# Attention and two MoE layers on one core: the first MoE in three passes instead of four

## The chip, the cores and the metric

The kernel runs on one core of a Trainium2 chip. The metric is the device time of one execution in microseconds (us), here the median of three runs. The engines are named as in the profile: PE (TensorE, matmuls), PEld (its weight loads), DVE (VectorE), ACT (ScalarE), POOL (GpSimd), and SP, whose queue issues nearly all DMA transfers.

## What is computed

Block-causal attention over 4 batches of 576 tokens with 8 heads of 64, then a gated layer over all 2304 tokens, then four experts whose outputs are weighted by probabilities. All of it is float32 (the first layer's weights come as float64).

```python
def _attn_ref(q, k, v):                    # q, k, v: (4, 8, 576, 64)
    scores = scale * np.matmul(q, k.transpose(0, 1, 3, 2))
    mask = block_i >= block_j              # blocks of 64 positions
    scores = np.where(mask, scores, -1000000000.0)
    ...                                    # softmax over the last axis
    return np.matmul(attn, v)

def _moe_ref(x, w_gate, w_val, w_out):     # x: (2304, 512), d_ff 1536
    gate = 1.0 / (1.0 + np.exp(-(x @ w_gate)))
    return gate * (x @ w_val) @ w_out

def _moe2_ref(x, domain_probs, w1, w2):    # 4 experts, 512 -> 1024 -> 512
    p = domain_probs / (domain_probs.sum(-1, keepdims=True) + 1e-09)
    for e in range(E):
        out += p[:, e:e + 1] * (np.maximum(x @ w1[e], 0.0) @ w2[e])
    return out
```

## The kernel before

**Numbers.** A float32 factor is split into a high and a low part (`split_sb`: one engine rounds, another subtracts), and a product is three matmuls: high by high, high by low, low by high. First products are done by a Winograd scheme: 2 x 2 blocks of x and of the weights, seven block products instead of eight, with sums of blocks made beforehand.

**Stages.** (1) Attention, `attn_items` (L152), makes a queue of small steps for each batch and pair of heads: loads, transposes of q and k (`prep_tr`, L224), scores, softmax, transposes of the probabilities, product with v (`pv_both`, L511). It writes its result to DRAM tiles `x_d[batch, "a" or "b", pair]`: "a" has the first 256 tokens of the batch, "b" the other 320. Batches 0 and 1 are of kind N (scores from unsplit factors), 2 and 3 of kind F (split factors).
(2) The first MoE, in `NP1` = 4 passes p of 576 tokens, each two halves t of `TH1` = 288. Twelve steps f run over blocks of 128 gate and 128 value columns (d_ff 1536). A step has one first product, `l1_1` (L788): seven block products of 6 matmuls in the order 1, 2, 6, 5, 7, 4, 3, into banks c1 and c2, with copies (`snap`), additions and the gate behind them, and at its end the tile g. Two steps share a second product, `l2_1` (L865): 4 output blocks x 2 halves x 2 steps x 3 matmuls, added into x2 tiles by DVE (L884), in banks "lo" and, from pass 2 on, "o". It runs among the matmuls of the next two steps. After the last step the x2 tiles are written to DRAM (`x2_d`).
(3) The second MoE, in three passes of 768 tokens (halves of 384): first products `l1_items`, second products `l2_items` (pass 0, 512 columns) and `l2s_items` (later passes, 256 columns).

**What a pass needs.** `x1_prep(p)` (L736) or, for passes 2 and 3, `x1_early` loads the blocks of x of batch p, makes four sums on POOL and splits seven blocks into the xc tiles. `w1_load(f)` loads the split weights of a step: tiles a, b, c of tag "wg" (6 of them in a ring) and d. In pass 0 the weights come in float64; `conv_items(f)` makes them and stores them to DRAM. `wo_get` does the same for w_out (4 whole tiles). All tiles of the first MoE lie in one pool, `moe1`; a pool for pass 2's early x (`x1b`) lies where attention was.

**Order.** The outer loop over passes (L1297) lists the steps' items, puts loads between them as side items, merges them with the second product of the two steps before (`_merge`), and before each item asks for attention up to a place: `attn_to(A1[p] + (A1[p+1] - A1[p]) * share / PACE1)`, where a place counts batches (1.05 is batch 0 and a twentieth of batch 1). With `A1 = [1.05, 2.3, 4, 4, 4]` pass 0 takes batch 1 and 0.3 of batch 2, pass 1 the rest. This order is a priority: the Tile framework schedules the instructions of each engine by it and by a timeline of its own, so that work stated later can run earlier where its inputs and tiles are free.

Of the kernel before, what the change touches and what calls it, by code (L numbers as in the profile page):

```python
# [21 lines left out]
A1 = [1.05, 2.3, 4, 4, 4]  # L22
PACE1 = 0.9
GB = 4
UB = 1
# [9 lines left out]
W2B = 4  # L35
FIRSTP = 1
W1B = 5
PRE0, PRE1 = 0.4, 0.9
# [24 lines left out]
def attention_moe_moe_kernel(  # L63
# [72 lines left out]
    moe1 = tc.alloc_tile_pool(name="moe1", bufs=1)  # L136
# [15 lines left out]
    def attn_items(segs):  # L152
# [6 lines left out]
        QTS = KTS = {"N": range(5), "F": range(5)}  # L159

        def nat_of(g):
            return pairs[g][3] != "F"
# [20 lines left out]
        def load(g, nm, src, c0, c1):  # L183
# [14 lines left out]
            for x, (y, z) in enumerate(((nm, src),) if nm == "v" else (("k", k), ("q", q)) if nm == "k" else ()):  # L198
                nc.sync.dma_start(
                    out=t[64 * x:64 * x + 64, 4], in_=z[b, 2 * pr:2 * pr + 2, 512:S, :].rearrange("h p d -> p h d"))  # L200
# [6 lines left out]
        def loads(g):  # L207
            load(g, "q", q, 0, 4)
            load(g, "k", k, 0, max(kts_of(g)) + 1)
# [60 lines left out]
        first = sum(x[3] != "F" for x in pairs)  # L270
# [4 lines left out]
        for g, pair in enumerate(pairs):  # L275
# [3 lines left out]
            if pair[3] == "F":  # L279
# [10 lines left out]
        order = {"N": 0, "F": 0}  # L290
# [251 lines left out]
        def prep_list(g):  # L542
            seg = pairs[g][3]
            r = [(False, 0.0, lambda: prep_alloc(g))]
            for nm, cs in (("q", range(4)), ("k", KTS[seg])):
# [12 lines left out]
        for g in range(len(pairs)):  # L558
# [5 lines left out]
            later(base + per // 2, (g, False, 0.0, lambda g=g: load_v(g)))  # L564
# [47 lines left out]
    NP1 = B  # L612
    TP1 = S
    TH1 = TP1 // 2
    QF = 2 * P
    KH = NKT // 2
    C1 = TH1 / 2.4 + 2.6
# [3 lines left out]
    wo_d = [dram.tile([P, 2, DM], F32, name=f"wod{i}") for i in range(NF)]  # L621
# [3 lines left out]
    def w1_tile(k):  # L625
        n = 1 if k == "d" else 2
        return moe1.tile([P, 2, n, QF], F32R, tag="wd" if k == "d" else "wg", name=f"w{k}", bufs=2 if k == "d" else 6)
# [48 lines left out]
    def wo_get(p, f):  # L676
        t = wo[f] = moe1.tile([P, 2, DM], F32R, tag="wo", name="wo", bufs=4)
        if p:
            nc.sync.dma_start(out=t.bitcast(F32), in_=wo_d[f])
# [3 lines left out]
        split_sb(t[:, 0], t[:, 1], from_f64(raw), "a", "p")  # L683
        nc.sync.dma_start(out=wo_d[f], in_=t.bitcast(F32))
# [3 lines left out]
    def end_bank():  # L688

        n = nb1["end"] = nb1.get("end", -1) + 1  # L690
        tag = ("lo", "o", "s", "t")[n % 4]
# [11 lines left out]
    def winograd_left(pool, dst, load, n):  # L703
# [7 lines left out]
        def s(kk, m):  # L711
            if m in (1, 3):
                d[kk, "s", m] = pool.tile([P, n], F32, tag=f"xs{m}", name="xs")
# [22 lines left out]
    def x1_prep(p):  # L736
        def load(kk, t, h):
            kt = h * KH + kk
            r = moe1.tile([P, TH1], F32, tag="xr1", name="xr1", bufs=4)
            while (p, "b", kt) not in x_d:  # L740
                attn_next()
            if t == 0:
                nc.sync.dma_start(out=r[:, :QA], in_=x_d[p, "a", kt])
                nc.sync.dma_start(out=r[:, QA:], in_=x_d[p, "b", kt][:, :TH1 - QA])
            else:
                nc.sync.dma_start(out=r, in_=x_d[p, "b", kt][:, TH1 - QA:])
            return r

        return winograd_left(moe1, xc1, load, TH1)

    def x1_early(p, pool):

        d = {}
        n = TH1

        def load(t, h):
            r = d[t, h] = pool.tile([P, KH, n], F32, tag=f"xb{t}{h}", name="xb")
            for kk in range(KH):
                kt = h * KH + kk
                while (p, "b", kt) not in x_d:  # L760
                    attn_next()
                if t == 0:
                    nc.sync.dma_start(out=r[:, kk, :QA], in_=x_d[p, "a", kt])
                    nc.sync.dma_start(out=r[:, kk, QA:], in_=x_d[p, "b", kt][:, :n - QA])
                else:
                    nc.sync.dma_start(out=r[:, kk], in_=x_d[p, "b", kt][:, n - QA:])

        def s(m):
# [665 lines left out]
```

## Time and profile before

| what | value |
|---|---|
| runs | 1416.87, 1419.59, 1421.7 us; median 1419.59 |
| the profiled execution | 1417.34 us, its span 1415.6 us |
| busy in the span | PE 97%, PEld 89%, DVE 69%, ACT 55%, POOL 34% |
| DMA | 371.93 MB moved, 263 GB/s |
| attention and conversion before the first MoE | 0 to 72 us |
| pass 0, first matmul of the first product | 72 us |
| pass 1, the same | 289 us |
| pass 2, pass 3, the same | 462 and 563 us |
| second MoE | from 680.5 us |

The profile is of one execution. An engine's busy time is the time in which it had an instruction under way; PE's matmuls overlap, so their mean duration is longer than the time from one to the next. What a matmul costs in a row of others is read from a stretch that has no other work: its length by its number of matmuls. The granted clock is the share of TensorE's full clock that was given.

### The profile page before, as it was taken

What the parts mean: (1) busy time and instruction counts of PE and PEld (TensorE: products, weight loads), DVE (VectorE), ACT (ScalarE), POOL (GpSimd) and SP (SyncE); (2) the same over time, 40 slices, a digit from 0 to 9 for tenths busy, and PEclk for the clock granted to TensorE, in tenths of its full rate; (3) what the DMA queues carried; (4) which work ended last, traced back from release to release, by engine and by line L of the source; (5) the groups of instructions that cost most, each with busy time, mean ns of one, the idle gap of its engine ahead of it and who ended that gap; (6) DMA issues with size and microseconds to landing.
All of it is one profiled execution on the core that took longest, in us unless ns stands there. A gap on an engine that the chain in (4) does not pass through costs nothing.

```text
span 1415.6 us, 26232 instructions
## 1 busy us (share of the span) xinstructions
PE 1373.8 (97%) x9212; PEld 1266.7 (89%) x9212; DVE 983.1 (69%) x2103; ACT 780.7 (55%) x1926; POOL 480.4 (34%) x502
## 2 busy tenths in 40 slices
PE   5889999999999999999999999999999999999998
PEld 3447788889899999999999989989999999999998
DVE  6867789986766445467777666757766687766766
ACT  5878788888876433343445445445444454443442
POOL 4544345312112100012576556533322342322322
PEclk8989999999999999999999999999999999999999
DMA  7988787767756888898799888886676777676754
GB/s 227 311 243 277 218 278 264 246 204 214 217 178 229 306 296 267 282 364 311 264 336 358 296 300 302 281 308 227 226 254 249 249 266 278 246 269 231 276 205 157
DMA packets 213683, 371.93 MB, mean 263 GB/s; under 512 B 75568, under 2 KB 140080, under 8 KB 207408
## 3 DMA queue, kind: packets, MB, share of 16 engines
q1 hardware_dynamic: 212464, 369.99, 77.1%
q8 instruction: 74, 1.21, 0.3%
q14 instruction: 57, 0.47, 0.1%
q10 hardware_dynamic: 1088, 0.26, 0.1%
HBM read 269.00 MB, written 101.19 MB: 262 GB/s over the span
## 4 chain that ended last, share of the span: by engine, by line
PE 83%; DMA 5%; DVE 5%; ACT 3%; issue 2%; SPq 1%; POOL 1%; DVEq 0%; ACTq 0%; POOLq 0%
PE c L119 37%; PE o L119 25%; PE lo L119 7%; PE s L119 4%; PE obank L119 3%; PE t L119 2%; PE tbank L458 2%; DMA raw<-in_moe_w_out_dram 1%; DMA raw<-in_moe_w_gate_dram 1%; PE s L349 1%; DMA wa<-w1d 1%; ACT pt L382 1%; DMA w1g<-w1d 1%; PE tbank L229 1%; POOL wt L653 1%
## 5 line engine op out<-in xcount | busy, mean ns | idle before, releaser
L119 PE MATMUL c<-xc,w1g 128*128 128x384 f32 x1920 | 384.8, 338 | 2.1 <-DMA w1g<-w1d 1.8
L119 PEld LDWEIGHTS c<-xc,w1g 128*128 128x128 f32 x1920 | 330.4, 188 | 8.8 <-DVE hb L1062 1.3
L119 PE MATMUL o<-w2s,hb 128*128 128x256 f32 x1728 | 243.5, 282 | 1.1 <-DVE acc L1211 1.1
L119 PEld LDWEIGHTS o<-w2s,hb 128*128 128x128 f32 x1728 | 231.8, 189 | 2.0 <-DVE acc L1211 1.7
L1211 DVE SCALAR_TENSOR_TENSOR acc<-o,pr_t,acc 128x256 f32<-128x256 f32 x264 | 123.4, 479 | 57.9 <-PE o L119 55.7
L1071 POOL TENSOR_TENSOR hs<-hf 128x384 f32<-128x384 f32 x64 | 64.1, 1023 | 287.1 <-ACT hf L1079 255.7
L119 PE MATMUL lo<-g,wo 128*128 128x288 f32 x888 | 148.0, 300 | 4.8 <-DVE x L884 4.8
L119 PE MATMUL o<-w,hb 128*128 128x512 f32 x576 | 142.9, 391 | 0.0
L119 PEld LDWEIGHTS lo<-g,wo 128*128 128x128 f32 x888 | 125.8, 188 | 9.6 <-DVE x L884 6.7
L1079 ACT ACTIVATE hf<-c 128x384 f32<-128x384 f32 x128 | 65.7, 513 | 115.7 <-DVE c L1116 58.4
L119 PEld LDWEIGHTS o<-w,hb 128*128 128x128 f32 x576 | 107.2, 188 | 18.5 <-DVE acc L1155 0.3
L1116 DVE TENSOR_TENSOR c<-c,snap 128x384 f32<-128x384 f32 x144 | 77.9, 553 | 55.8 <-PE c L119 38.9
L1109 ACT ACTIVATE snap<-c 128x384 f32<-128x384 f32 x144 | 65.8, 485 | 85.6 <-PE c L119 85.4
L1060 ACT ACTIVATE hb<-hs 128x384 fp32r<-128x384 f32 x128 | 63.3, 518 | 65.0 <-POOL hs L1071 64.9
L1062 DVE TENSOR_TENSOR hb<-hs,hb 128x384 fp32r<-128x384 f32 x128 | 87.1, 695 | 5.8 <-ACT hb L1060 5.4
L884 DVE TENSOR_TENSOR x<-lo,x 128x288 f32<-128x288 f32 x124 | 55.6, 452 | 45.6 <-PE lo L119 45.0
L119 PE MATMUL c<-xc,wa 128*128 128x288 f32 x504 | 82.6, 299 | 0.9 <-DMA wa<-w1d 0.5
L382 ACT ACTIVATE pt<-s,nm 128x128 f32<-128x128 f32 (+3 forms) x128 | 67.4, 530 | 17.2 <-DVE nm L380 14.5
L119 PEld LDWEIGHTS c<-xc,wa 128*128 128x128 f32 x504 | 71.2, 188 | 3.1 <-DMA wa<-w1d 0.8
L119 PE MATMUL c<-xc,wc 128*128 128x288 f32 x432 | 71.0, 299 | 1.1 <-ACT snap L808 1.1
L458 PE MATMUL tbank<-ident,pt 128*128 128x128 f32 x320 | 55.3, 287 | 17.2 <-ACT pTa L445 9.9
L808 ACT ACTIVATE snap<-c 128x288 f32<-128x288 f32 x108 | 44.2, 409 | 43.8 <-PE c L119 43.2
(173 smaller groups left out, 2697.5 us busy)
## 6 DMA issues: line engine op xcount, KB each, us to landing
w1g<-w1d SPq DMA_DIRECT2D x96, 512.0 KB, 5.4
w2s<-w2d SPq DMA_DIRECT2D x48, 1024.0 KB, 6.5
w1d<-w1g SPq DMA_DIRECT2D x48, 512.0 KB, 5.0
wa<-w1d SPq DMA_DIRECT2D x40, 512.0 KB, 5.2
wb<-w1d SPq DMA_DIRECT2D x40, 512.0 KB, 5.3
wc<-w1d SPq DMA_DIRECT2D x40, 512.0 KB, 4.4
wo<-wod SPq DMA_DIRECT2D x36, 512.0 KB, 6.0
wr<-in_moe_w_dram SPq DMA_DIRECT2D x32, 512.0 KB, 5.4
```

The lines of the kernel that those rows point to most:

```text
L119: ins = nc.tensor.matmul(out=out, lhsT=lhsT, rhs=rhs, start=start, stop=stop, skip_group_check=skip)
L382: ins = nc.scalar.activation(out=pt[:, x * nk:(x + 1) * nk], in_=sp[:, x - x0], func=AF.Exp, bias=nm[:, j0 + x:j0 + x + 1], scale=1.0, acc ...
L458: nc.tensor.transpose(out=tbank[:, x * P:(x + 1) * P], in_=pt[:, x * P:(x + 1) * P], identity=ident)
L808: nc.scalar.activation(out=t, in_=d["c1"][:, :TH1], func=AF.Copy)
L884: nc.vector.tensor_tensor(out=x2[t, dm], in0=ps, in1=x2[t, dm], op=ALU.add)
L1060: nc.scalar.activation(out=t[:, 0], in_=src, func=AF.Copy if low is None else AF.Relu)
L1062: nc.vector.tensor_tensor(out=t[:, 1], in0=src, in1=t[:, 0].bitcast(F32), op=ALU.subtract)
L1071: nc.gpsimd.tensor_tensor(out=o, in0=x, in1=y, op=op)
L1079: nc.scalar.activation(out=hf[q, blk], in_=c, func=AF.Relu)
L1109: nc.scalar.activation(out=t, in_=d["c1"][:, :TH], func=AF.Copy)
L1116: nc.vector.tensor_tensor(out=c, in0=d[tag][:, :TH], in1=d[n], op=ALU.add)
L1211: nc.vector.scalar_tensor_tensor(out=o, in0=ps, scalar=pr, in1=o, op0=ALU.mult, op1=ALU.add)
```

## The change

The first MoE runs in three passes of 576, 832 and 896 tokens. The halves are `N1 = (288, 416, 448)` columns, and `X1` says of which pieces of batches a half is made. Pass 1 has batch 1 and the first 256 tokens of batch 2, pass 2 the rest of batch 2 and batch 3. For that, attention of batch 2 is two segments: G with query and key blocks 0 and 1, and H with the others. G's keys and values of blocks 0 and 1 are loaded, and the keys transposed, for H again. The places become `A1 = [1.05, 3.05, 5, 5]`.

Instead of one pool there are several: weights (`wts`, ring of 5 instead of 6 tiles, w_out in 6 half tiles instead of 4 whole ones), and for each pass `mg` (g and x2), `mx` (xc) and `my` (the other tiles, `snap` 2 instead of 3). The loads and sums of x stand in tiles that the gates use later (`room`). A pass's pools are released when it ends, and those of the next take their place, with waits by tile. Pass 2's inputs are made in the last two steps (`XE`) of pass 1, where attention was.

The last second product of pass 0 is not merged with pass 1's first steps: `go(prev, [])` states it behind pass 0, in banks lo, c1 and c2 by turns. The second product's loop runs over output blocks first and halves second.

For the second MoE, `p2r` is allocated on the left and `p2` on the right; x of its pass 0 is loaded into tiles of other tags; the five w1g tiles are shared out to the two pools (2 and 3), and the block c of weight tile 0 and all of tile 1 are prepared behind the first MoE instead of in its last pass.

The diff, cut:

```diff
-A1 = [1.05, 2.3, 4, 4, 4]
-PACE1 = 0.9
+A1 = [1.05, 3.05, 5, 5]
+PACE1 = (1.0, 0.9, 0.9)
 GB = 4
+WGB = 5
+WOB = 6
+SNB = 2
...
-        QTS = KTS = {"N": range(5), "F": range(5)}
+        QTS = {"N": range(5), "F": range(5), "G": range(2), "H": range(2, 5)}
+        KTS = {"N": range(5), "F": range(5), "G": range(2), "H": range(5)}
...
-    NP1 = B
-    TP1 = S
-    TH1 = TP1 // 2
+    N1 = (288, 416, 448)
+    O1 = (0, 576, 1408)
+    NP1 = len(N1)
+    X1 = (((0, "a", 0, 256), (0, "b", 0, 32)), ((0, "b", 32, 320),)), \
+         (((1, "a", 0, 256), (1, "b", 0, 160)), ((1, "b", 160, 320), (2, "a", 0, 256))), \
+         (((2, "b", 0, 320), (3, "a", 0, 128)), ((3, "a", 128, 256), (3, "b", 0, 320)))
...
-        t = wo[f] = moe1.tile([P, 2, DM], F32R, tag="wo", name="wo", bufs=4)
+        ts = wo[f] = [wts.tile([P, 2, QF], F32R, tag="wo", name="wo", bufs=WOB) for _ in range(2)]
...
-    def end_bank():
+    def end_bank(p):
...
+        n = nb1["end", p] = nb1.get(("end", p), -1) + 1
+        tag = (("lo", "c1", "c2") if p == 0 else ("lo", "o", "s", "t"))[n % (3 if p == 0 else 4)]
...
-            r = moe1.tile([P, TH1], F32, tag="xr1", name="xr1", bufs=4)
+            if p == 2:
+                r = room(("xr", kk), 4)[:, 2 * t + h]
+            elif kk == 0:
+                r = room(("c", t), 2)[:, h]
+            elif t == 0:
+                r = room(("r",), 2)[:, h]
             else:
+                r = room(("snap", h), 1)[:, 0]
+            o = 0
+            for b, g, c0, c1 in X1[p][t]:
+                while (b, g, kt) not in x_d:
+                    attn_next()
+                nc.sync.dma_start(out=r[:, o:o + c1 - c0], in_=x_d[b, g, kt][:, c0:c1])
+                o += c1 - c0
...
+        if p == 1:
+            for m in (3, 4, 7, 6, 2, 5, 1):
+                xc1.setdefault(p, {})[m] = xcp[p].tile([P, 2, KH, n], F32R, tag=f"xc{m}", name=f"xc{m}")
...
-                d["o"] = m_bank(p, "lo") if (p, n0) != (NP1 - 1, NF - 2) else end_bank()
+                d["o"] = m_bank(p, "lo") if n0 != NF - 2 or p == 1 else end_bank(p)
...
-        for t in (1, 0):
-            for dm in range(NKT):
+        for dm in range(NKT):
+            for t in (1, 0):
...
-        queue = attn_items([(0, "N"), (1, "N"), (2, "F"), (3, "F")])
+        queue = attn_items([(0, "N"), (1, "N"), (2, "G"), (2, "H"), (3, "F")])
...
-                    pre = x_prep(0) + [(0.0, lambda: (w_load(0), w_load(1), p_prep()))] + wp[0] + wp[1][:-2] + [(0.0, lambda: w2_load(0))]
+                    pre = x_prep(0) + [(0.0, lambda: (w_load(0), w_load(1), p_prep()))] + wp[0][:6] + wp[0][7:] + [(0.0, lambda: w2_load(0))]
...
                 prev = l2_1(p, f0)
+                if f0 == NF - 2 and p < NP1 - 1:
+                    my[p].release()
+                    mx[p].release()
+                    if p == 0:
+                        go(prev, [])
+                        prev = []
+                        mg[0].release()
+                        mg[1] = tc.alloc_tile_pool(name="mg1", bufs=1, reuse_waits="tile")
+                        mx[1] = tc.alloc_tile_pool(name="mx1", bufs=1, reuse_waits="tile")
+                        my[1] = tc.alloc_tile_pool(name="my1", bufs=1, reuse_waits="tile")
+                        xcp[1] = mx[1]
...
         w2_load(1)
+        run(wp[0][6:7] + wp[1])
```

## Rows read from the trace of the kernel before

**Rows 1.** The page: busy time by engine, and slices of 35 us with granted clock.
```profile
PE 1373.8 (97%) x9212; PEld 1266.7 (89%) x9212; DVE 983.1 (69%) x2103; ACT 780.7 (55%) x1926; POOL 480.4 (34%) x502
...
PE   5889999999999999999999999999999999999998
...
PEclk8989999999999999999999999999999999999999
```

**Rows 2.** Windows: stretch, length; busy (instructions) of PE, PEld, DVE, ACT, POOL; clock, DMA, GB/s.
```profile
72.35:125.00 52.65, 45.49 (x278) 28.78 (x277) 35.78 (x97) 40.01 (x121) 24.74 (x27) 0.90 0.85 253
...
210.00:289.00 79.00, 73.93 (x539) 65.97 (x538) 72.31 (x170) 67.01 (x183) 35.58 (x36) 1.00 0.78 252
289.00:325.00 36.00, 34.81 (x252) 30.82 (x252) 30.07 (x88) 30.80 (x92) 3.23 (x6) 1.00 0.72 213
...
480.00:560.00 80.00, 80.00 (x606) 80.00 (x605) 39.56 (x79) 28.07 (x65) 0.00 (x0) 1.00 0.80 276
560.00:600.00 40.00, 39.03 (x290) 38.31 (x290) 22.11 (x43) 16.24 (x38) 1.02 (x1) 1.00 0.84 281
...
680.00:720.00 40.00, 39.75 (x208) 36.42 (x207) 28.10 (x42) 22.02 (x44) 26.10 (x28) 1.00 0.97 339
720.00:920.00 200.00, 200.00 (x1003) 181.21 (x1003) 140.87 (x212) 100.22 (x199) 118.30 (x128) 1.00 0.89 309
960.00:1160.00 200.00, 200.00 (x1415) 200.00 (x1413) 141.24 (x283) 88.72 (x197) 63.06 (x58) 1.00 0.70 248
```

**Rows 3.** Waits of PE from 210 to 330 us: total us, times, longest.
```profile
PE lo L119 <- DVE x L884: 4.4, 5, 1.4
```

**Rows 4.** Windows around the stretch of lower granted clock, columns as in Rows 2.
```profile
94.00:97.50 3.50, 1.81 (x9) 0.58 (x7) 3.22 (x10) 3.01 (x11) 1.01 (x1) 1.00 0.89 192
97.50:107.80 10.30, 9.62 (x37) 5.29 (x38) 7.20 (x21) 7.51 (x22) 6.32 (x7) 0.50 0.63 192
```

**Rows 5.** Timeline of PE: start, length, group; a run lasts until the next start.
```profile
674.94 5.72 PE L119 MATMUL lo<-g,wo 128*128 128x288 f32 x42
680.50 3.68 PE L119 MATMUL c<-xc,w1g 128*128 128x384 f32 x20
...
701.54 4.24 PE L119 MATMUL o<-w,hb 128*128 128x512 f32 x18
705.62 0.56 PE L119 MATMUL c<-xc,w1g 128*128 128x384 f32 x2
...
802.16 2.80 PE L119 MATMUL c<-xc,w1g 128*128 128x384 f32 x15
804.79 1.53 PE L119 MATMUL o<-w,hb 128*128 128x512 f32 x6
...
1060.44 1.58 PE L119 MATMUL o<-w2s,hb 128*128 128x256 f32 x12
1061.86 0.33 PE L119 MATMUL c<-xc,w1g 128*128 128x384 f32 x1
```

**Rows 6.** Groups of instructions: transposes of key blocks.
```profile
L229 PE MATMUL tbank<-ident,kn 128*128 128x128 f32 x80 | 15.6, 296 | 1.1 <-ACT tqn L237 0.5 <-ACT pTb L445 0.5
```

**Rows 7.** The path of x: groups with busy us, mean ns; transfers with median us.
```profile
L133 DVE TENSOR_TENSOR xc<-xs,xc 128x384 fp32r<-128x384 f32 x24 | 14.0, 584 | 7.3 <-ACT xc L131 7.2
...
L718 POOL TENSOR_TENSOR xs<-xr,xs 128x384 f32<-128x384 f32 x6 | 6.4, 1060 | 12.3 <-DVE xc L133 12.3
...
xd2a<-xr SPq DMA_DIRECT2D x4, 128.0 KB, 2.7
...
xr<-xd1a SPq DMA_DIRECT2D x4, 128.0 KB, 2.5
```

**Rows 8.** Timeline of SP from 96 to 102 us: issues of DMA transfers.
```profile
97.58 0.45 SPq L743 DMA_DIRECT2D xr<-xd0a  x1
...
99.55 0.38 SPq L746 DMA_DIRECT2D xr<-xd0b  x1
```

**Rows 9.** DMA issues of the first MoE's weights, columns as in Rows 7.
```profile
wa<-w1d SPq DMA_DIRECT2D x40, 512.0 KB, 5.2
```

More of the change, by code (lines that the diff above doesn't have):

```diff
@@ L35 @@
 W2B = 4
+XE = 2
 FIRSTP = 1
 W1B = 5
+W1P = 2
 PRE0, PRE1 = 0.4, 0.9
@@ L207, in loads @@
         def loads(g):
-            load(g, "q", q, 0, 4)
+            load(g, "q", q, min(QTS[pairs[g][3]]), min(max(QTS[pairs[g][3]]) + 1, 4))
             load(g, "k", k, 0, max(kts_of(g)) + 1)
@@ L268, in last_q @@
                     out=w[64:128, r], in0=src[r], scalar=SCALE, in1=w[0:64, r].bitcast(F32), op0=ALU.mult, op1=ALU.subtract)
-        first = sum(x[3] != "F" for x in pairs)
+        first = sum(x[3] == "N" for x in pairs)
         seq, start = [], []
@@ L563, in attn_items @@
                 later(base, (g, False, 0.0, lambda g=g: loads(g)))
-            later(base + per // 2, (g, False, 0.0, lambda g=g: load_v(g)))
+            free = 0 if g < 2 else start[g - 2] + 5 if pairs[g - 2][3] == "G" else start[g - 1] - 1 + LP
+            later(max(base + per // 2, free), (g, False, 0.0, lambda g=g: load_v(g)))
             pl = prep_list(g)
@@ L701, in attention_moe_moe_kernel, with winograd_left @@
     xc1 = {}
-    def winograd_left(pool, dst, load, n):
+    def winograd_left(pool, dst, load, sums, n):
         r = []
@@ L712, in s @@
             if m in (1, 3):
-                d[kk, "s", m] = pool.tile([P, n], F32, tag=f"xs{m}", name="xs")
+                d[kk, "s", m] = sums(kk, m)
             o = d[kk, "s", 3 if m == 3 else 1]
@@ L736, in x1_prep, with room @@
     def x1_prep(p):
+        n = N1[p]
+        keep = {}
+        def room(key, m):
+            if key not in keep:
+                pool, tag = (xst, key[0]) if p == 2 else (my[p], key[0])
+                keep[key] = pool.tile([P, m, n], F32, tag=tag, name="xr1", bufs=dict(c=2, snap=SNB).get(tag, 1))
+            return keep[key]
         def load(kk, t, h):
             kt = h * KH + kk
-            r = moe1.tile([P, TH1], F32, tag="xr1", name="xr1", bufs=4)
-            while (p, "b", kt) not in x_d:
-                attn_next()
@@ L925, in load, with sums, w1_room @@
                 return a
-            return winograd_left(p2r, xc, load, TH)
+            def sums(kk, m):
+                if p:
+                    return p2.tile([P, TH], F32, tag=f"xs{m}", name="xs")
+                if (kk, "s") not in keep:
+                    keep[kk, "s"] = p2r.tile([P, 4, QF], F32, tag="wt", name="xs").rearrange("p a d -> p (a d)")
+                x = int(m == 3)
+                return keep[kk, "s"][:, x * TH:(x + 1) * TH]
+            return winograd_left(p2r, xc, load, sums, TH)
+        w1n = [0]
+        def w1_room():
+            w1n[0] += 1
+            x = (w1n[0] - 1) % W1B
+            pool, n = (p2r, W1P) if x < W1P else (p2, W1B - W1P)
+            return pool.tile([P, 2, 2, QF], F32R, tag="w1g", name="w1g", bufs=n)
         wq = {}
```

186 lines of the change are left out of this document (83 added, 103 removed).

## Prediction


> **What bounds the kernel now.** I read the page's busy shares and slices first: PE is busy 97% of the span, and from the fourth slice on nine tenths or more [rows 1]. A busy PE need not be one at its peak, so the second view is the windows by stage, in which each stretch gives a time per matmul [rows 2]. From 480 to 560 us only the first MoE runs: 606 matmuls of 288 columns in 80.00 us, 132.0 ns each, no idle time. So there the number and the length of the matmuls make the time, and DVE, ACT, POOL and DMA have room. The places where PE idles are few: 72 to 125 us (45.49 busy of 52.65), the end of the first pass (73.93 of 79.00, then 34.81 of 36.00), and a little at each change of pass [rows 2]. The waits view puts most of the idle time around the end of the first pass on the single bank "lo" of the second product, which waits for the DVE addition: 4.4 us in 5 waits [rows 3]. Last, in one stretch, 97.5 to 107.8 us, the granted clock is 0.50, the lower of the two levels, after a stretch in which PE was busy 1.81 of 3.50 us [rows 4].
>
> **Part A, fewer and longer matmuls.** A pass issues 12 x (42 + 24) = 792 matmuls of half its tokens each. Before: four passes of 288 columns, 3168 matmuls x 132.0 ns = 418.2 us. After: three passes of 288, 416 and 448 columns, the same columns in 2376 matmuls. The second MoE has runs at other lengths [rows 5]: 12 of 256 in 1.42 us (118.3 ns), 15 of 384 in 2.63 us (175.3), 18 of 512 in 4.08 us (226.7). Between the last two, 416 columns take 188.2 ns and 448 take 201.0. Sum after: 792 x (132.0 + 188.2 + 201.0) = 412.8 us, **5.4 us less**. A line through 256 and 512 has 0.423 ns for a column and 9.9 ns for a matmul; by it the gain is 792 x 9.9 = 7.8 us. I take 5.4, as 384 and 512 lie nearest; their mixed window, 1003 matmuls in 200 us at 84 of 384 to 72 of 512, gives 199.4 ns at a mean of 443 columns, and so agrees [rows 2]; the window of 256 and 384 (1415 in 200 us) is of the same kind.
>
> The Trainium skill ("TensorE: Matmul & The Clock Gate", section "Wait — 56ns, not 53.3ns?") states a fixed cost of about 2.5 ns for each matmul at the full clock; by that the gain would be an estimated 2.0 us and the rest of the distance would go with columns. The rows of three lengths speak against it: what is left at zero columns is 9.9 ns, not 2.5.
>
> **Part B, batch 2 in two halves.** Segment G (query and key blocks 0 and 1) and H (the rest) need key blocks 0 and 1 transposed twice: 2 x 4 pairs = 8 more transposes. 80 of this kind keep PE busy for 15.6 us [rows 6], so **+1.6 us**; their copies lie on ACT and DVE beside matmuls. Scores, transposes of probabilities and the products with v are the same instructions, moved. Up to the end of pass 0 the order asks for the same amount of attention as before (batch 1 and about a quarter of batch 2), so pass 0 isn't made denser; the remaining 1.7 batches spread over a pass half as long again.
>
> **Part C, one change of pass less.** From 560 to 600 us, the change from pass 2 to 3, 290 matmuls took 40.00 us where 290 x 132.0 ns is 38.3 [rows 2]: **-1.7 us** (1.0 by idle time alone). The change from pass 1 to the last one remains, with its inputs loaded over two steps instead of early ones; its pool lies where attention was and waits only for that. I take 0, bounds -1 and +2.
>
> **Part D, the change from pass 0 to 1.** The last second product of pass 0 no longer runs among first products of the next pass but behind pass 0 alone, in three banks. That a tail alone can run without loss shows at the end of the first MoE: 42 matmuls from 674.94 to 680.50 us, 132.4 ns each [rows 5], in four banks, with earlier second products kept back to cover the last gate. Three banks leave 1.6 us (12 matmuls) for one addition, so the single-bank waits don't come back here. But pass 1 now needs tokens of batch 2: the last pair of G goes out to DRAM (2.7 us), back (2.5) [rows 7], then through two sums on POOL (about 1.1 each at 384 columns) and a split (DVE 0.58, about as much on ACT): some 8.6 us, with multiplication and issue about 10, before the third step can start; and the loads stand in tiles that the gates take over, so the first gate waits for all four sums. Cover: half a tail (24 x 132.0 ns = 3.2 us), two steps (12 x 188.2 = 2.3 us) and what attention of H can be put there. That leaves about 4.5 us in which PE has attention alone; in the stretch from 72 to 125 us, mostly attention, PE was 86% busy [rows 2], so 0.6 us is lost, and some of the tail's own. The change was not free before: 1.2 us idle from 289 to 325 us. Taken **+1.5 us**, bounds -1 and +10 (next part but one).
>
> **Part E, the loads of pass 0.** Before, four load tiles made the second half of x's blocks wait for the first: SP issued the loads of batch 0's second block at 97.58 us together with those of the last one [rows 8]. With a tile for each half all but the last pair's are issued before. Three of six loads (0.5 us of SP each) and two splits leave this stretch: **-1.5 us**, bounds -4 (the half-clock stretch goes, too) and +2 (the gates wait for the tiles that hold the loads).
>
> **Part F, into the second MoE.** Block c of the first weight tile and most of the second's move behind the last first product: some 5 splits and 4 sums beside a tail of 48 x 201.0 ns = 9.6 us, with room for them in the freed inputs. From 680 to 720 us PE was busy 39.75 of 40.00 us [rows 2]. **+0.5 us**, bounds 0 and +2.
>
> **Taken at nothing.** Twelve fewer weight loads of each kind (40 of 512 KB, 5.2 us each to landing [rows 9]): no wait of weight worth speaking of is seen, so nothing is gained. The ring goes from 6 tiles to 5: a slot is still freed two thirds of a step ahead (8.8 us of 13.3 in pass 2), more than 5.2. If that cover went, each of 12 steps would show the remainder. Fewer evacuations: those engines aren't the bound. SP's queue: the half tiles of w_out add issues, and one that waits for its slot holds back what stands behind it, the weights of the next step, which have the same lead.
>
> **Sum.** -5.4 + 1.6 - 1.7 + 1.5 - 1.5 + 0.5 = **-5.0 us**. The profiled execution took 1417.3 us (span 1415.6 and 1.7 around it): 1412.3 us. The median of the three runs is 2.3 above it, but their range (1416.9 to 1421.7) holds it; I leave the number at 1412.3. About 0.3%, 4.3 us, is what can be told from no change, so this forecast lies just past it.
>
> **Rivals.** (1) *The fixed cost is the line's and the changes of pass are clean*: -7.8 + 1.0 - 1.7 + 0 - 2.5 + 0 = -11 us, **1406.3**. For it: three lengths on one line. Against it: 384 lies above the line.
> (2) *Slower: PE runs dry at the change from pass 0 to 1.* Place: the third step of pass 1, behind the last pair of G. If attention of H can't be put there, the 4.5 us are all idle, and the gate's wait for two more sums adds 2.2. Then the stretch of half clock comes again: 10.3 us [rows 4] in which about half is lost, 5 us. Instead of +1.5 that is +12: -5.0 + 10.5 = +5.5 us, **1422.8**. It decides as soon as an idle time there is as deep as that from 94 to 97.5 us. For it: the chain through DRAM is real. Against it: instructions are put in order by a list scheduler, which kept work back in the tail at 675 us.
> (3) *No difference: pass 0 gives back.* Room for w_out falls from four blocks to three, so a half of it waits for the end of a second product, and holds one of three raw tiles meanwhile. From 210 to 289 us PE already idles 5.1 us [rows 2]; if the last two pairs wait 2 us more each: **1416.3**.
> (4) *No difference: the time beyond the columns goes with the columns.* Then A gives nothing: **1417.7**. For it: 132.0 / 288 = 0.458 ns and 199.4 / 443 = 0.450 ns a column are close. Against it: 118.3 / 256 = 0.462 and 226.7 / 512 = 0.443, so a column does cost more in a shorter matmul [rows 2, 5]. The page of the Trainium skill named under A points this way.
> (5) *It doesn't do what it says*: if tiles of the new pools waited for whole pools, passes would not overlap; each wait is by tile, so I give it no chance of its own.
>
> **How the numbers follow.** Forecast 0.40 (1409 to 1413), rival 1 0.15, rival 2 0.20, rival 3 0.20, rival 4 0.05. Faster is the first two, 0.55; slower rival 2, 0.20; within 0.3% the rest, 0.25. Range: low end the good bounds, -7.8 + 1.0 - 2.7 - 1 - 4 = -14.5, 1403; high end rival 2 with the bounds of C and F on top (+2.3), 1425.
>
> **What would show it.** A: a stretch of pass 2 with about 201 ns a matmul and one of pass 1 with about 188 where no attention is left. B: 88 transposes of kn. C: no idle time in the middle of the last pass. D: the granted clock and idle PE behind pass 0's last second product; an idle time over 4 us or a clock of 0.5 there is rival 2. E: loads of xd0 tiles issued between 70 and 95 us, and whether the clock still falls. F: PE idle at the first steps of the second MoE. Wrong would be the prediction if pass 0 itself got longer, or if 448 columns took 205 ns or more.

## The result and the profile after

The changed kernel takes **1440.70 us** (median of 4 runs, 1435.41 to 1442.64) against 1419.87 us before (1416.87 to 1421.70): a ratio of **1.0143**, 95% interval 1.0111 to 1.0175. It is slower by some 21 us, where the forecast was 5.0 us less than the profiled execution before (1412.3 us), and lies above the range. The profiled execution is the shortest of the four (1435.41 us, span 1433.6), so the trace shows 18.0 us of the loss.

The page of the kernel after answers to [rows 1]: PE's busy time by engine, its slices of 36 us, and the granted clock. PE is busy for 6.2 us more than before, with 784 matmuls fewer, and the fourth and the eighth slice (107 to 143 and 251 to 287 us) are a step lower.

```profile
PE 1380.0 (96%) x8428; PEld 1246.9 (87%) x8428; DVE 980.2 (68%) x2011; ACT 784.0 (55%) x1874; POOL 485.7 (34%) x514
...
PE   5888999899999999999999999999999999999998
...
PEclk8989999999999999999999999999999999999999
```

The windows of the kernel after, columns as in [rows 2]: the first stretch of the first MoE, the one behind it, the change from pass 0 to 1, that from 1 to 2, a part of the last pass, and the way into the second MoE.

```profile
72.35:125.00 52.65, 42.94 (x254) 26.78 (x253) 32.96 (x92) 36.66 (x113) 20.97 (x25) 0.90 0.71 206
...
125.00:205.00 80.00, 74.55 (x517) 58.77 (x516) 59.10 (x145) 62.57 (x182) 26.21 (x29) 1.00 0.73 229
...
290.00:345.00 55.00, 50.74 (x325) 43.64 (x324) 44.03 (x114) 45.26 (x124) 9.76 (x11) 1.00 0.76 207
...
480.00:540.00 60.00, 57.36 (x300) 52.48 (x299) 35.19 (x52) 31.34 (x57) 10.44 (x8) 1.00 0.60 192
...
580.00:660.00 80.00, 80.00 (x388) 72.66 (x388) 42.88 (x65) 27.98 (x52) 11.91 (x11) 1.00 0.62 199
680.00:720.00 40.00, 38.58 (x197) 35.32 (x196) 25.20 (x36) 14.62 (x29) 17.61 (x18) 1.00 0.72 251
```

From 72 to 125 us PE is busy 42.94 us where [rows 2] have 45.49, with 254 instructions in place of 278. In the next 80 us it idles 5.45 us; the kernel before has there

```profile
125.00:205.00 80.00, 78.86 (x556) 64.13 (x553) 62.29 (x155) 65.82 (x183) 27.72 (x29) 1.00 0.77 248
```

1.14 us. So PE gets less done in pass 0; that pass 0 itself got longer is what the prediction named as one of the things that would make it wrong. The second MoE is the same: from the last second product of the first MoE to the end of the span it is 735.0 us, before 734.9.

The granted clock still falls in pass 0, but not for longer than before: it is at the lower of its two levels in these two stretches, 10.4 us together, against one of 10.3 us before [rows 4]. Ahead of the first PE was busy 1.77 of 3.50 us, ahead of the second 1.52 of 3.50. So a longer stretch of half clock is not the difference.

```profile
80.60:87.50 6.90, 6.37 (x25) 3.61 (x23) 2.49 (x10) 4.42 (x16) 0.45 (x1) 0.51 1.03 350
104.50:108.00 3.50, 3.50 (x14) 2.44 (x14) 3.05 (x10) 2.94 (x9) 2.22 (x3) 0.51 0.02 5
```

To sort the loss by pass I took, from the start times of all PE instructions, the time from each to the start of the next, and counted what exceeds the median for its shape as lost; the medians times the counts are the work. Pass 0 ends here with its last second product, the first MoE with its own last one. In us (the medians of attention's shapes move by a few us between kernels, so work and loss of a line are good to about 3 us, their sum is exact):

| | before | after | own load tiles | the same, 2 tiles for the last pass's loads |
|---|---|---|---|---|
| profiled span | 1415.6 | 1433.6 | 1425.8 | 1420.8 |
| matmuls of the first MoE, work | 421.4 | 419.0 | 415.9 | 415.9 |
| attention, work | 203.8 | 204.8 | 209.1 | 208.7 |
| lost up to the first product | 25.5 | 25.7 | 25.7 | 26.1 |
| lost in pass 0 | 27.4 | 39.1 | 29.5 | 25.8 |
| lost in the rest of the first MoE | -0.7 | 6.5 | 6.3 | 5.1 |

The two columns on the right are experiments, below. Of the kernel after's loss, 11.7 us lie in pass 0 and 7.2 in the rest, most of that at the two changes of pass.

The chain in pass 0 stands in the timeline of the kernel after (start, length, engine, group): the last pair of x loads, the last sum, the first snap and the first gate.

```profile
96.87 0.86 SPq L777 DMA_DIRECT2D xr<-xd0b  x2
...
116.22 0.80 POOL L735 TENSOR_TENSOR xr<-xr,xr 128x288 f32<-128x288 f32 x1 [1.49 <-DVE xc L138]
...
112.83 0.41 ACT L815 ACTIVATE snap<-c 128x288 f32<-128x288 f32 x1
...
118.96 0.45 DVE L818 TENSOR_TENSOR r<-c,snap 128x288 f32<-128x288 f32 x1
```

The first gate (r) comes at 118.96 us, 1.9 us behind the end of the last of the input's sums. In the kernel before it came 7 us earlier, and the sums went on beside it:

```profile
111.81 0.46 DVE L811 TENSOR_TENSOR r<-c,snap 128x288 f32<-128x288 f32 x1
...
117.14 1.01 POOL L718 TENSOR_TENSOR xs<-xr,xr 128x288 f32<-128x288 f32 x1
```

That is the wait that part E had as its bad bound: c, r and snap are now the tiles into which x is loaded, and t the one in which it is summed.

### The profile page after: what moved, and what is told of

It reads as the page before. It is cut to its first block, busy times and chain, and to the rows that moved or that the text cites. A ratio compares the mean times of both kernels' runs of the same rounds, so it can differ in the third digit from the quotient of the medians.

```text
span 1433.6 us, 24464 instructions
## 1 busy us (share of the span) xinstructions
PE 1380.0 (96%) x8428; PEld 1246.9 (87%) x8428; DVE 980.2 (68%) x2011; ACT 784.0 (55%) x1874; POOL 485.7 (34%) x514
## 4 chain that ended last, share of the span: by engine, by line
PE 81%; DVE 7%; DMA 5%; ACT 3%; issue 2%; SPq 1%; POOL 1%; ACTq 0%; DVEq 0%; POOLq 0%
PE c L124 37%; PE o L124 24%; PE lo L124 7%; PE s L124 4%; PE obank L124 3%; PE t L124 2%; PE tbank L468 2%; DMA raw<-in_moe_w_val_dram 2%; PE s L359 1%; DVE raw L618 1%; ACT pt L392 1%; DMA raw<-in_moe_w_out_dram 1%; DVE xc L138 1%; PE tbank L239 1%; DVE raw L617 1%
## 5 line engine op out<-in xcount | busy, mean ns | idle before, releaser
L124 PE MATMUL lo<-g,wo 128*128 128x288 f32 (+2 forms) x744 | 152.7, 339 | 7.2 <-DVE x L892 7.2
L892 DVE TENSOR_TENSOR x<-lo,x 128x288 f32<-128x288 f32 (+2 forms) x104 | 55.8, 542 | 42.9 <-PE lo L124 42.4
L124 PE MATMUL c<-xc,wa 128*128 128x288 f32 (+2 forms) x396 | 81.2, 340 | 3.0 <-DVE xc L138 1.7
L124 PEld LDWEIGHTS c<-xc,wa 128*128 128x128 f32 x396 | 66.7, 188 | 8.1 <-DVE xc L138 2.2
L815 ACT ACTIVATE snap<-c 128x288 f32<-128x288 f32 (+2 forms) x90 | 43.2, 481 | 55.2 <-PE c L124 51.0
L124 PE MATMUL c<-xc,wc 128*128 128x288 f32 (+2 forms) x360 | 73.0, 337 | 0.3 <-ACT snap L815 0.3
```

The lines of the kernel that those rows point to most:

```text
L124: ins = nc.tensor.matmul(out=out, lhsT=lhsT, rhs=rhs, start=start, stop=stop, skip_group_check=skip)
L815: nc.scalar.activation(out=t, in_=d["c1"][:, :n1], func=AF.Copy)
L892: nc.vector.tensor_tensor(out=x2[t, dm], in0=ps, in1=x2[t, dm], op=ALU.add)
```

## The experiments

All times are medians; ratios are to the kernel before as run beside them (its medians: 1417.0 to 1418.5 us).

**The pace of attention.** The kernel after asks for segments G and H by places that don't go with their cost. My first theory was that this crowds the first half of pass 0. One run makes the places of the kernel after go with cost; the other gives the kernel before the uneven demand.

```
-A1 = [1.05, 3.05, 5, 5]
+A1 = [1.05, 2.28, 4, 4]        # and place: G counts 0.24, H 0.76 of one
```

> The changed kernel with one thing altered: a place counts attention by its cost, so that G is 0.24 and H 0.76 of batch 2 and pass 0 asks for batch 1 over 68 to 75% of its length, as before, not over the first 47%. Theory T1 (uneven demand): pass 0 lost about 10 us in its first half because two thirds of its attention were asked for in under half of its matmuls; this kernel takes 1429 to 1433 us against 1440.7, and its first 200 us have some 44 us of PE time lost over the pace of its forms as before, not 54. Theory T2 (scarcer tiles: 5 weight tiles, 2 snaps, w_out in three blocks): no change, 1438 to 1442. A mixture: in between.

Measured: 1441.05 us, ratio 1.0165 (1.0147 to 1.0182).

```
 attn_to(...)                    # kernel before, pass 0, s = share of the pass
+  1.05 + 2 * s if s < 0.475 else 2 + 0.5 * (s - 0.475)
```

> The kernel before with one thing altered: in pass 0 it asks for attention by the changed kernel's rule (batch 1 done at 47.5% of the pass, then a quarter of batch 2 over the rest). T1: slower by 8 to 12 us, 1428 to 1432, with the loss between 72 and 210 us. T2: as before, within 3 us of 1419.9.

Measured: 1418.26 us, ratio 1.0010 (0.9995 to 1.0025). No gain in the one, no loss in the other: the theory falls.

**Less room.** The change makes three rings smaller. The prediction took the weights (6 tiles to 5) at nothing, did not speak of snap (3 to 2), and had w_out (4 blocks to 3) as a rival. First the kernel before with the two smaller rings, together and each alone.

```
-bufs=2 if k == "d" else 6      # weights
+bufs=2 if k == "d" else 5
-tag="snap", name="snap", bufs=3
+tag="snap", name="snap", bufs=2
```

> The kernel before with the changed kernel's rings: 5 weight tiles instead of 6 and 2 snaps instead of 3. T1: within 2 us of before. T2: 3 to 8 us slower, with waits of first products for snap and for weights.

Measured: 1426.47 us, 1.0060 (1.0039 to 1.0081).

> The kernel before with 5 weight tiles instead of 6 and nothing else. The run with this and 2 snaps took 9.2 us more. If weights are the cause: 1423 to 1428; if snaps: 1416 to 1420; if both: 1420 to 1423.

Measured (weights alone): 1422.51 us, 1.0041 (1.0026 to 1.0056).

> The kernel before with 2 snaps instead of 3 and nothing else. If snaps are the cause of the 9.2 us: 1423 to 1428, with first products waiting for DVE and snap; if weights: 1416 to 1420.

Measured (snap alone): 1420.04 us, 1.0029 (1.0014 to 1.0044). So room has a price in the kernel before. The counter-test gives the kernel after its old room back in pass 0:

```
+ex0 = tc.alloc_tile_pool(name="ex0", bufs=1)   # a 6th weight tile, a 4th w_out block; snap 3
```

> The changed kernel with the room of before given back in pass 0 alone, from memory that is free there: a sixth weight tile, a third snap, a fourth block of w_out (two more half tiles). T2 (scarce tiles make pass 0 longer; 9 us each for rings and w_out in the kernel before): 1425 to 1431 against 1440, with some 10 us less before the first matmul of pass 1. Rival T4 (the loss lies with the shape of the passes itself: gates that wait for load tiles, the tail, 448 columns): 1437 to 1441.

Measured: 1440.21 us, 1.0164 (1.0142 to 1.0185). There more room gives nothing back.

**Half tiles of w_out.** The kernel before with half tiles and the other order of the second product, then with as many halves as there was room, then with that order alone.

```
-t = wo[f] = moe1.tile([P, 2, DM], ..., bufs=4)
+ts = wo[f] = [moe1.tile([P, 2, QF], ..., bufs=6) for _ in range(2)]   # 8 in the second run
-for t in (1, 0):
-    for dm in range(NKT):
+for dm in range(NKT):
+    for t in (1, 0):
```

> The kernel before with the changed kernel's w_out: 6 half tiles (three blocks of room instead of four), split and stored by halves, and output blocks as the outer loop of the second product. T1: within 2 us of before. T2 (and the prediction's third rival): 3 to 8 us slower, as a raw tile of the conversion is held until the second product of two steps ago ends; the loss lies in pass 0.

Measured: 1426.89 us, 1.0062 (1.0045 to 1.0078).

> The kernel before with w_out in half tiles and the second product's new loop order, but with 8 of them, the room of before. If the room is the cause of the 9.7 us of the run with 6: 1416 to 1420, as before. If the split into halves (24 more instructions and 12 more stores in pass 0, and twice the loads) or the loop order is: 1424 to 1428.

Measured: 1427.43 us, 1.0065 (1.0044 to 1.0087).

> The kernel before with the second product's loop over output blocks first and halves second, w_out whole and nothing else altered. If the loop order is the cause of the 10 us in the two runs with half tiles: 1424 to 1429. If the halves are (more instructions, stores and loads): 1415 to 1419.

Measured: 1417.22 us, 0.9993 (0.9980 to 1.0006). Neither the room nor the order, but the halves themselves cost 10 us in the kernel before. The windows from 120 to 205 us of the run with the order alone and, behind it, of that with 8 halves show where:

```profile
120.00:205.00 85.00, 83.31 (x580) 67.12 (x579) 65.62 (x166) 70.28 (x198) 29.60 (x32) 1.00 0.78 252
```

```profile
120.00:205.00 85.00, 77.04 (x536) 61.82 (x534) 62.19 (x155) 67.95 (x194) 29.34 (x34) 1.00 0.78 247
```

PE is busy 6.3 us less, with ACT, DVE and POOL no busier: not the length of the added splits. What it waits for there is an evacuation of attention and one of the gates' additions:

```profile
PE tbank L458 <- ACT pTb L445: 2.1, 1, 2.1
PE c L119 <- DVE c L814: 2.1, 2, 1.1
```

In the run with the order alone the longest wait of that stretch is 0.6 us. The other way round, whole tiles in the kernel after:

```
-ts = wo[f] = [wts.tile([P, 2, QF], ..., bufs=WOB) for _ in range(2)]
+t = wo[f] = wts.tile([P, 2, DM], ..., bufs=3)
```

> The kernel after with only the half tiles of w_out undone (three whole tiles); x loads and sums stay in the tiles of the gates. If the two losses add up (theory H and the shared tiles): 1440.7 - 10 = 1431 us. If the halves cost nothing in the kernel after (theory N): 1440 us. If whole tiles pay here by more than in the run with own x tiles, the wait of the gates is what the split and stores of w_out run into.

Measured: 1436.49 us, 1.0128 (1.0108 to 1.0148): 4.2 us less by the medians, with overlapping intervals; not the 10 us. But its profile differs from that of the kernel after in where the time is lost: by the count of the table about 30 us in pass 0 instead of 39, and 13 in the rest of the first MoE instead of 6.5; the second MoE takes 739.8 us instead of 735.0. And the first gate still comes as late as in the kernel after, right behind the last sum:

```profile
116.46 1.32 POOL L732 TENSOR_TENSOR xr<-xr,xr 128x288 f32<-128x288 f32 x1 [2.63 <-DVE xc L138]
118.06 0.45 DVE L815 TENSOR_TENSOR r<-c,snap 128x288 f32<-128x288 f32 x1
```

So the late gate by itself does not make the whole loss of pass 0. (Part of the difference may be the clock: in this run's pass 0 it is at half for 3.4 us, in the kernel after for 10.4.)

**The load tiles.** The kernel after with own tiles for the x loads and the sums of pass 0, then with four load tiles instead of eight and the room of the earlier run, then with own load tiles alone.

```
+x0p = tc.alloc_tile_pool(name="x0p", bufs=1)
+if p == 0:                     # in load
+    r = x0p.tile([P, n], F32, tag="xr1", name="xr1", bufs=8)
+if p == 0:                     # in sums
+    return x0p.tile([P, n], F32, tag=f"xs{m}", name="xs")
```

> The changed kernel in which the loads and sums of x of pass 0 get tiles of their own (as before the change) instead of the tiles that the gates take over. Theory T5 (the first gate waits for the last sum: in the changed kernel it is written at 119.0 us, 7.2 us later than before, and the first step ends at 126 instead of 122.5): the first gate near 112 us and the whole 4 to 8 us shorter, 1433 to 1437. Rival (that delay is filled with attention and costs nothing): 1438 to 1442.

Measured: 1428.13 us, 1.0063 (1.0044 to 1.0082).

> The last kernel with the room of before in pass 0 as well (sixth weight tile, third snap, fourth block of w_out). If both, scarce tiles and shared load tiles, add up: 1425 to 1431. If room does nothing here, as in the run with room alone: as the run with own load tiles.

Measured: 1431.10 us, 1.0084 (1.0061 to 1.0107).

> Half of the edit of the own x tiles: the eight loads of pass 0 have own tiles, the two sums of each kk stay in the tile of tanh ('t', one buffer). If the gates wait for the loads' tiles (c, r, snap): about 1428, as with both. If it is the one tile of the sums that holds the second half of the inputs and the first gate: about 1440, as without. In between, both have a share.

Measured: 1426.79 us, 1.0067 (1.0048 to 1.0085). So own load tiles alone give back 11 to 14 us (by ratio and by median), over half of the loss, and more than the 4 to 8 us expected. Own sums add nothing to that; nor does more room, in a run that has four load tiles instead of eight. Its timeline (POOL and DVE) has the last sum at 113.05 us and the first gate before it, not behind it:

```profile
113.05 0.92 POOL L736 TENSOR_TENSOR xr<-xr,xr 128x288 f32<-128x288 f32 x1 [1.82 <-DVE xc L138]
...
109.53 0.46 DVE L821 TENSOR_TENSOR r<-c,snap 128x288 f32<-128x288 f32 x1 [0.33 <-PE c L124]
```

and its windows are near those of the kernel before: 45.70 of 52.50 us and 77.97 of 80.

```profile
72.50:125.00 52.50, 45.70 (x287) 29.86 (x283) 34.63 (x99) 40.31 (x126) 24.16 (x30) 0.93 0.80 237
125.00:205.00 80.00, 77.97 (x542) 63.44 (x542) 59.63 (x155) 63.78 (x182) 27.67 (x30) 0.98 0.71 230
```

**What a matmul of 448 columns takes.** A kernel of its own issues 96 matmuls of each of several lengths back to back, some of them twice, from rows of two strides.

```
+cases = [(512, 512), (256, 256), (288, 288), ..., (448, 448), ..., (448, 512), ..., (448, 448)]
```

> Not the function: it writes zeros, and runs 16 products of 6 matmuls for each of 16 cases of length and row stride, one after the other, with copies on ACT beside them. In the changed kernel 416 columns took 188 ns as the line from 384 to 512 has it, but 448 took 206.5 instead of 201. If this is of the length itself (a step between 416 and 448), 448 takes 206 here, at either stride. If it is the row stride of 1792 bytes: 206 at stride 448 and 201 at stride 512. If it is the company (other engines' work): 201 here. At zero columns a line through 256 and 512 leaves 9.9 ns in the kernel before; here 8 to 14.

Its timeline of PE (start, length of the run of 96):

```profile
32.19 11.68 PE L94 MATMUL b256x<-x,w 128*128 128x256 f32 x96
43.71 12.96 PE L94 MATMUL b288x<-x,w 128*128 128x288 f32 x96
56.50 16.81 PE L94 MATMUL b384x<-x,w 128*128 128x384 f32 x96
73.15 17.75 PE L94 MATMUL b400x<-x,w 128*128 128x400 f32 x96
90.74 18.30 PE L94 MATMUL b416x<-x,w 128*128 128x416 f32 x96
108.88 18.95 PE L94 MATMUL b432x<-x,w 128*128 128x432 f32 x96
127.67 19.99 PE L94 MATMUL b448x<-x,w 128*128 128x448 f32 x96
147.49 20.25 PE L94 MATMUL b464x<-x,w 128*128 128x464 f32 x96
...
209.99 21.94 PE L94 MATMUL b512x<-x,w 128*128 128x512 f32 x96
231.76 19.61 PE L94 MATMUL b448x<-x,w 128*128 128x448 f32 x96
251.21 18.25 PE L94 MATMUL b416x<-x,w 128*128 128x416 f32 x96
269.30 12.80 PE L94 MATMUL b288x<-x,w 128*128 128x288 f32 x96
281.94 19.61 PE L94 MATMUL b448x<-x,w 128*128 128x448 f32 x96
```

Start to start, divided by 96: 133.2 ns for 288 columns, 173.4 for 384, 189.0 for 416; 448 take 206.5 ns the first time and 202.6 the second. The third time, from 281.94 us and with rows of the first stride again, the run is 19.61 us long, like the second. The stride is not it.

**What is left of the loss.** Whole w_out tiles on top of own loads and sums:

> The run with own x tiles in pass 0 (1428.13 us, 1.0063 of the kernel before), and in it the half tiles of w_out are undone: three whole tiles, one split pair, one store and one load for each f block, as before; the order of the second product (both t of a dm after each other) stays. Theory H (the halves cost the kernel after what they cost the kernel before, where they were worth 1427.43 - 1417.22 = 10 us): about 1418, a ratio of 0.999 to 1.002. Theory N (the halves cost only where the ring of four blocks and four passes stand around them; what is left of the loss lies at the changes of pass and in the 448 columns): 1426 to 1429, as without the edit. In between, each has a share.

Measured: 1433.35 us, 1.0107 (1.0085 to 1.0129), 5 us more than with half tiles, worse than both theories. So the halves have no price of their own that carries over, and neither have the shared load tiles: beside whole w_out tiles, own loads and sums give back 3 us (1436.49 to 1433.35, with overlapping intervals), not 11 to 14. In pass 0 about 28 us are lost, against 30 with shared tiles. So either edit, own load tiles or whole w_out tiles, takes some 10 us out of pass 0, and the second adds little; why that is, and why whole tiles lose time behind pass 0, is not shown. The same with attention of pass 0 asked for earlier:

```
-PACE1 = (1.0, 0.9, 0.9)
+PACE1 = (0.9, 0.9, 0.9)
```

> The kernel with own x tiles and whole w_out, and in pass 0 the attention is asked for at a pace of 0.9 instead of 1.0, so that segment G is ready about a tenth of pass 0 (24 us) earlier. If what is left at the change from pass 0 to 1 (about 5 us more than in the kernel before) is the chain of the last pair of G through DRAM, it goes: 3 to 5 us less than without this edit. If it lies in the sums and splits behind the last gate of pass 0, or if denser attention costs pass 0 as much, nothing: within 1.5 us of the run without this edit.

Measured: 1440.04 us, 1.0145 (1.0123 to 1.0167): 7 us worse. The edit did not do what it was made for: the last pair of G is stored at 251.5 us, without the edit at 247.4. So this run says nothing about an earlier G. Both last runs show a stretch of half clock behind the change from pass 0 to 1, as rival 2 had it; in the first of them:

```profile
310.00:318.90 8.90, 7.43 (x48) 5.40 (x47) 7.62 (x20) 7.58 (x21) 3.45 (x3) 1.00 0.94 245
318.90:329.10 10.20, 9.31 (x32) 7.51 (x32) 8.32 (x27) 8.82 (x27) 3.14 (x4) 0.50 0.43 112
```

The last two go back to own load tiles alone, and take one change of pass each: two tiles in place of one for the loads and sums of the last pass, and x of batch 0 in place of batch 2 in pass 1, so that nothing waits for G's trip through DRAM.

```
-bufs=dict(c=2, snap=SNB).get(tag, 1)
+bufs=dict(c=2, snap=SNB, xr=2, xs=2).get(tag, 1)
```

> The kernel with own load tiles in pass 0 (1426.8 us, ratio 1.0067), and two tiles instead of one for the loads and for the sums of the last pass, so that the second half of its x blocks is loaded without waiting for the sums of the first half. Around that change of pass PE has about 6 us of time beyond what its matmuls take there (480 to 540 us), against 1.5 at the change from pass 1 to 2 of the kernel before. If the one tile makes it: 1422 to 1425 us, ratio 1.0035 to 1.0055. If it is the chain of sums and splits itself, beside gates of three engines: 1426 to 1428, no change.

Measured: 1424.17 us, 1.0037 (1.0025 to 1.0049).

```
-((1, "b", 160, 320), (2, "a", 0, 256))
+((1, "b", 160, 320), (0, "a", 0, 256))
```

> The kernel with own load tiles in pass 0, and pass 1 takes the first block of batch 0 in place of that of batch 2 as its x (so part of its result is that of other tokens; all instructions stay, and segment G is still made). The loads of pass 1 then don't wait for the last pair of G, which goes through DRAM. If that chain makes the loss at the change from pass 0 to 1 (about 6 us beyond the matmuls from 280 to 320 us, 1.6 of it in the kernel before): 1421 to 1424 us, ratio 1.003 to 1.005. If the loads wait for the tiles of the gates of pass 0 to be free, or the sums and splits for their engines: 1426 to 1428, no change.

Measured: 1424.35 us, 1.0048 (1.0032 to 1.0064). The windows of the two changes of pass, of the run with own load tiles, of that with two tiles, and of that with old x:

```profile
280.00:320.00 40.00, 36.89 (x227) 31.76 (x226) 32.23 (x80) 30.69 (x81) 9.05 (x8) 0.96 0.76 221
480.00:540.00 60.00, 56.71 (x291) 49.79 (x290) 36.82 (x59) 28.20 (x56) 11.49 (x10) 1.00 0.60 192
```

```profile
280.00:320.00 40.00, 36.61 (x228) 30.72 (x227) 34.15 (x82) 33.17 (x89) 9.04 (x8) 1.00 0.78 227
480.00:540.00 60.00, 56.30 (x292) 50.40 (x291) 35.93 (x56) 28.44 (x55) 12.71 (x10) 1.00 0.64 200
```

```profile
280.00:320.00 40.00, 36.64 (x222) 30.55 (x222) 34.41 (x83) 33.18 (x87) 8.78 (x8) 1.00 0.75 217
```

Neither edit makes PE idle less in its own stretch (3.1, 3.4 and 3.4 us at the first change; 3.3 and 3.7 at the second). From the end of pass 0 to the last second product the run with old x takes 388.3 us, that with own load tiles 388.2. So G's trip through DRAM is not what the first change waits for, which the prediction had as its price. The queue of the kernel after says the same: the last pair of G is stored 31 us before the first of pass 1's loads is issued (18 us in the run with own load tiles), and that first load is of batch 1.

```profile
260.25 1.18 SPq L550 DMA_DIRECT2D xd2a<-xr  x1
...
291.36 0.43 SPq L777 DMA_DIRECT2D xr<-xd1a  x1
```

Two tiles do put the second half of the last loads forward: behind the first half there is a gap of 1.5 us (499.74 to 501.20 us) instead of 9.5 (503.22 to 512.72), and that stretch, 387.0 us, is 1.2 us shorter; the medians and ratios, 2.6 to 4 us, are on that side, and the two intervals just overlap. The remainder of the difference between these three profiles lies in pass 0, before either edit acts. There DVE, ACT and POOL do the same instructions in the same order in all three, and still 29.5, 25.8 and 25.1 us are lost, with 13.7, 6.8 and 0 us of half clock: so much can lie between two executions of the same work, and as much of the two gains cannot be put down to the edits.

What makes the 3 us at each change I could not settle. One rival stands in the traces and no run tests it: the loads of pass 1 still share the tiles of its gates, and in the kernel after the first gate of pass 1 follows its last sum at once:

```profile
322.52 1.10 POOL L735 TENSOR_TENSOR xr<-xr,xr 128x416 f32<-128x416 f32 x1 [3.06 <-DVE xc L138]
...
323.66 0.59 DVE L818 TENSOR_TENSOR r<-c,snap 128x416 f32<-128x416 f32 x1
```

The other is the sums and splits themselves, beside the gates of three engines.

## Why the prediction was wrong

**Part E, the step that failed.** It took -1.5 us for the x loads of pass 0, with a bad bound of +2 for gates that wait for the tiles that hold the loads. The loads did move forward: of the twelve, seven are issued by 69.1 us and the last three at 93.84 to 97.30, where in the kernel before three were out by then and the last six began at 97.58 [rows 8]. The term was mis-sized, and so was its bound: in the kernel after, sharing the load tiles costs 11 to 14 us, and with own load tiles the time lost in pass 0 falls from 39.1 us to between 25.1 and 29.5. I had priced the wait of one gate. The first gate does come 9 us later (118.96 against 109.53 us), and from 72 to 205 us PE did 771 instructions in place of 834. That the delay goes on through the bank that this gate frees and the products behind it is argued from the order of the kernel. It isn't the whole mechanism: with whole w_out tiles the gate is as late (118.06 us) and some 9 us of pass 0's loss are gone, so the price depends on w_out's halves too, which the prediction priced apart; how, is open. What the early loads are worth alone no run shows: with own load tiles again only three are out by 69.1 us, and 25.1 to 29.5 us lost against 27.4 before is -2.3 to +2.1.

**Part A.** Forecast -5.4. 288 and 416 columns took what was taken for them (133.2 and 189.0 in the length run, against 132.0 and 188.2). 448 were taken at 201.0 ns; in the kernel after 388 matmuls fill 80.00 us, 206.2 ns, so 792 of them are 4.1 us more, and the matmuls come to 2.4 us less by the table. In the run with own load tiles and two tiles for the last pass's loads the same stretch holds 397:

```profile
580.00:660.00 80.00, 80.00 (x397) 74.13 (x396) 44.70 (x73) 26.11 (x48) 8.88 (x9) 1.00 0.62 201
```

That is 201.5 ns, and the whole part is -5.5. So the size was right for one of two rates, and the kernel after ran at the other, past the 205 ns that the prediction had named as its limit.

**Part B.** 88 transposes of kn instead of 80, as said; attention's work is 1.0 us more in the kernel after and 4.9 in the table's last column; the split of work and loss, good to about 3 us, can hardly tell either from 1.6. That pass 0 is not made denser held as far as the two runs on pace can tell: the uneven demand cost nothing in either direction.

**Parts C and D**, -0.2 together, measured about +7 in the kernel after (6.5 lost in the rest of the first MoE against -0.7 in the kernel before) and +6 in the table's last column. The loss in the middle of the last pass went as said: from 580 to 660 us PE does not idle. D's +1.5 and C's 0 for the change from pass 1 to the last one were both too good: 4.3 and 2.6 us are idle at the changes in the kernel after (290 to 345 and 480 to 540 us) and some 3 us at each in the experiments, where the kernel before idles 1.2 us at the first [rows 2] and 0.55 us at the second (435 to 465 us). D's chain was the wrong one: without G's trip nothing is gained, and pass 1's loads begin long after it. Rival 2's half clock came in two of the experiments (10 and 14 us), for 3.4 us in a third, and not in the kernel after.

**Part F**, +0.5. PE idles 1.42 us from 680 to 720 us against 0.25 [rows 2], within its bounds; two waits for ACT's snap make it:

```profile
PE c L124 <- ACT snap L1139: 1.4, 2, 0.8
```

**Taken at nothing.** The kernel before pays for three small things: the weight ring of 5 costs 0.41%, though the prediction named a cover for it; the snap ring of 2, which it did not mention, 0.29%; the halves of w_out, of which it counted only the added issues and the room, 0.65%. In the kernel after none can simply be had back by undoing it: room gives nothing, and whole w_out tiles give 4 us there and lose 5 beside own load tiles. These parts don't add up; that each changes the order of ACT, DVE and POOL in the one crowded pass is the likely reason, which no run shows by itself.

**Rivals.** Rival 3 (pass 0 gives back, 4 us, by w_out's room) named the right pass, but not its cause: more room for w_out does nothing. Rival 2 had the right sign, but by its reason that was luck: its place, behind the last pair of G, holds none of the 11.7 us lost in pass 0, and its chain was done long before. Rival 1 had the changes of pass clean, and they were not. Rival 4, that time goes with columns, holds for 448 columns at the slower rate, at which the kernel after ran (206.2 / 448 is 0.460 ns a column, 132.0 / 288 is 0.458), and not at the faster one (201.5 / 448 is 0.450).

No version here is faster than the kernel before; the best is at 1.0037. Its remaining 5 us are, by the table, 5.8 more lost behind pass 0 and 4.9 more work of attention (good to 3 us), less 5.5 of the matmuls and 1.6 of pass 0; the rest, under 2 us, lies before the first product and in the second MoE.

**The range.** Its high end, 1425, put bounds of C and F at +2.3 on top of rival 2. Their own bounds come to +3.5 (C from 0 to +2, F from +0.5 to +2), and E's bad bound (+3.5 from its -1.5) and a slow rate of 448 columns (+4.1) were left out.

## What to carry to other kernels

When a load is put into a tile that a later step uses for something else, price the whole chain that ends in that tile's release (load, sum, split) against the first use, and then all that waits behind that use, not the load. Where PE already waits for ACT and DVE, parts that cost nothing by their own durations cost 3 to 14 us here and did not add, so undo one part at a time, in both kernels, and then pairs: own load tiles were worth 11 to 14 us beside half tiles of w_out and 3 beside whole ones. Before a chain is called the limit, compare the time at which its data are ready with the time at which their first user starts; here 31 us lay between. A length of matmul that no row shows needs a bound besides the line between its neighbours: 5 ns in 448 columns were 4.1 of the 5.4 us of the gain.

## What was not expected of the hardware

Matmuls of 448 columns run at one of two rates, 202 or 206 ns each, at full granted clock: in one kernel at both (127.67 and 231.76 us in the length run), between kernels at 388 or 397 in 80 us. Stride does not decide it; what does is open. What is left at zero columns depends on the runs that the line is drawn through: with 256 columns (11.52 us for 96, 120.0 ns) and 512 (226.8 ns) it is 13 ns, with the second run of 288 (12.64 us, 131.7 ns) and the same 512 it is 9.4, where the row that the forecast used left 9.9. The very first run, of 512 columns from 8.12 to 32.19 us, is left out: it took 250.7 ns a matmul at a granted clock of 1.00, and why is not known. The Trainium skill ("TensorE: Matmul & The Clock Gate", section "Wait — 56ns, not 53.3ns?") puts the fixed part at about 2.5 ns; no run here agrees with it, all of them with a weight load for each matmul.
